# Transformer layer with dilated local attention and SwiGLU FFN: zero products at the start, one pass and the output additions moved, new list priorities

## Chip, cores and metric

The kernel runs on one core of one Trainium2 chip. The metric is the device time of one execution in microseconds; the time of a kernel is the median of its runs. In the text PE is TensorE, ACT ScalarE, DVE VectorE, POOL GpSimd, SP the engine that issues DMAs.

## What is computed

One pre-norm transformer layer in float32, on a sequence of 2048 positions of width 640:

```python
h  = x + attention(layernorm(x)) @ wo          # 32 heads of 20, wqkv 640 x 1920
h2 = h + (silu(n @ w_gate) * (n @ w_up)) @ w_down   # n = layernorm(h), F = 1728
# attention: position t sees t, t-2, ..., t-14 (8 keys, dilation 2), softmax over those 8
```

Every float32 product is made of three passes on PE: an operand is split into a high part, rounded to PE's fp32r format, and a remainder (the low part), and the kernel adds high x high, high x low and low x high.

## The kernel before

**Tiles.** The sequence is cut into four blocks b of 512 rows, each of 4 sub-blocks j of 128; the width into 5 chunks c of 128 and, for attention, into 4 groups g of 8 heads.

**Stages.** (1) The first layer norm of b (`ln1`, `LnStats`): for b = 0 the first three sub-blocks are normalized on DVE (`one_dve`, L266 to L276), the fourth on ACT; PE transposes them (L361), ACT copies the result as the high part (L363), DVE makes the low part (L364). For other b the same is done by `x_columns` and `to_columns` (L313, L316, L317). (2) `load_wqkv` brings the weights, with ACT making high parts (L374) and DVE remainders (L376). (3) `qkv`: 15 products per (b, g, j) into one of PSUM banks 0 to 4 (L400); ACT copies them out (L405), and SP stores q, k, v to scratch tensors in HBM (L411, L420). (4) Attention on DVE per (b, g): k, v, q windows are loaded (L435, L440); products and sums over a head (L448, L453), softmax (L460 to L474, with the exponential on ACT, L466), weighted sum of v (L479, L487), a turn (L494) and a store (L500). (5) `wo`: the output projection, per b eight groups of 15 products (L569), with its inputs split on ACT (L558) and DVE (L559), then the residual (L575, L580) and the second layer norm. (6) `ln2_columns`: the normalized rows are transposed into the tile `shb`, in five groups of four transposes that use banks 7, 6, 5, 7, 6 in turn; each group's bank is read by the high copy (L316) and by the low subtraction (L317). For b = 3 this goes through DMA (`ln2_turn`). (7) `ffn`: 14 tiles of 128 columns; `load_ffn` brings and splits weights (L606 to L624), `proj` makes gate (bank 5) and up (bank 6) in three passes of five products (L630), then silu, product and split on ACT and DVE (L661 to L665), and `do_down` adds the down product into banks 0 to 4 (L642). (8) `finish`: five additions on DVE from banks 0 to 4 into the residual (L692, L696) and the output DMAs (L700).

The tile `shb` holds the QKV inputs of b = 1 and 3 first and the FFN inputs later, so the FFN of b = 0 can take it only behind the last QKV products of b = 3.

**What sets the order.** Nothing is issued as written. Each step calls `P.add` with its engine, an assumed cost, the regions that it reads and writes and a priority; `Plan.order` plays a list schedule over all of them with those costs, and issues every engine's steps in the order found. The engine takes the ready step with the lowest priority number. The numbers stand in the table `PR` (L33) or in the calls; attention's DVE steps have 20, PE's products 10. For a step with priority 20 or more the planner looks whether a more urgent one will be ready soon, and if so leaves the engine idle until then (L92 to L96). On the chip each engine runs its list in order and waits by semaphores, so a step that is planned too early stalls those behind it.

The steps of `order` and of `proj` before:

```python
soon = min((a for a, m in pend[e] if ops[m][4] == 1), default=1e9)
...
for p, (w, a) in enumerate(((0, 0), (0, 1), (1, 0))):
    P.add("PE", 1.145, ..., r=[rr(gu + 1280 * w, wid * NC), ("shb", 2560 * a, 2560 * a + 2560)], w=[pb(bk)], prio=10)
```

Of the kernel before, what the change touches and what calls it, by code (L numbers as in the profile page):

```python
# [10 lines left out]
F32 = mybir.dt.float32  # L11
# [20 lines left out]
LAT, LAT0, RATE = 4.0, 2.0, 350e3  # L32
PR = {'x': 6, 'wqd': 2.5, 'wqh': 3, 'wql': 2.5, 'qev': 1, 'kvs': 3, 'atl': 3, 'exp': 8, 'ost': 0.5, 'wod': 6, 'woh': 3, 'wol': 2, 'old': 1, 'fld': 3, 'lst': 3, 'wev': 1, 'fh': 2, 'fl': 8, 'ln1': 6, 't1': 2, 'wo0': 1.5, 'wo': 2}  # L33


class Plan:
# [23 lines left out]
    def order(self):  # L60
# [15 lines left out]
        while todo:  # L76
# [15 lines left out]
            if prio >= 20:  # L92
                soon = min((a for a, m in pend[e] if ops[m][4] == 1), default=1e9)
                if soon < t + ops[n][1] - 0.3:
                    free[e] = soon
                    continue  # L96
# [23 lines left out]
def dve(n):  # L120
    return 0.155 + 0.00104 * n
# [13 lines left out]
def program(tc, x_in, wqkv_in, wo_in, ffn_in, ffl_in, const_in, out):  # L135
# [7 lines left out]
    with tc.tile_pool(name="sb", bufs=1) as sb, tc.tile_pool(  # L143
# [12 lines left out]
        def h_t():  # L156
            if "h" not in late:
                late["h"] = sb.tile([128, 5120], F32, name="h", tag="sha")
            return late["h"]
# [42 lines left out]
        def f(o, n):  # L202
            return fa[:, o : o + n]
# [7 lines left out]
        def rr(o, n):  # L211
            return ("ra", o, o + n)

        def pb(i):
            return (f"b{i}", 0, 1)
# [104 lines left out]
        XH = 13440  # L320

        def wq(g, half, k):
            return 4800 * g + 2400 * half + 480 * k
# [13 lines left out]
        def ln1(b):  # L337
# [4 lines left out]
            if b:  # L342
# [7 lines left out]
                return  # L350
            for j in range(NJ):
                (st.one_dve if j < 3 else st.one)(j)
                for c0, n, bk, bo in ((0, 4, 7 - j % 2, 0), (4, 1, 5, j)):
# [171 lines left out]
        def wo(b, prio, bks):  # L525
# [18 lines left out]
            if b:  # L544
                P.add("SP", 0.6, lambda: Q.dma_start(h_t()[:, h0 : h0 + 2560], x_in[b].rearrange("p j c -> p (j c)")),
                      w=[("sha", h0, h0 + 2560)], prio=PR["old"], nbytes=nb(512, 2560))
            for j in range(NJ):
                jp = j // 2
                for i in range(3) if j % 2 == 0 else ():
# [76 lines left out]

        def proj(bk, gu, col, wid):
            def mm(p, w, a):
                for c in range(NC):
                    T.matmul(banks[bk], r_(gu + 1280 * w + wid * c + col, 128), x2(a, c), start=p == 0 and c == 0, stop=p == 2 and c == NC - 1)  # L630
            for p, (w, a) in enumerate(((0, 0), (0, 1), (1, 0))):
                P.add("PE", 1.145, lambda p=p, w=w, a=a: mm(p, w, a), r=[rr(gu + 1280 * w, wid * NC), ("shb", 2560 * a, 2560 * a + 2560)], w=[pb(bk)], prio=10)

# [10 lines left out]
        def ffn(b):  # L644
# [8 lines left out]
            for i in range(NF):  # L653
# [4 lines left out]
                if i < NF - 1:  # L658
                    proj(5, gu, 0, 256)
                    proj(6, gu, 128, 256)  # L660
                    P.add("ACT", act(512), lambda so=so: A.activation(f(so, 512), banks[5], AF.Silu), r=[pb(5)], w=[rf(so, 512)], prio=0, table="silu")  # L661
# [5 lines left out]
                else:  # L667
                    proj(5, gu, 0, 128)
                    P.add("ACT", act(512), lambda so=so: A.activation(fa[64:128, so : so + 512], banks[5][0:64, :], AF.Silu), r=[pb(5)], w=[rf(so, 512)], prio=0, table="silu")
# [9 lines left out]
        def finish(b):  # L679
# [7 lines left out]
            for j in range(NJ):  # L687
                cuts = (0, 256, 512) if b == NB - 1 and j == NJ - 1 else (0, 512)
                pieces = list(zip(cuts, cuts[1:]))[::-1]
                for o, e in pieces:  # L690
                    lo, hi = hsl(b, j, o, e - o)
                    P.add("DVE", dve(e - o), lambda lo=lo, hi=hi, o=o, e=e, j=j: V.tensor_add(h_t()[:, lo:hi], banks[j][:, o:e], h_t()[:, lo:hi]), r=[pb(j), ("sha", lo, hi)], w=[("sha", lo, hi)], prio=0)  # L692
                    if j == 0:
# [30 lines left out]


        load_x(0, (0,))
        P.add("SP", 0.45, lambda: Q.dma_start(f(MASK, 160), const_in), w=[rf(MASK, 160)], prio=0, nbytes=nb(128, 640))
        load_x(0, (1,))
# [88 lines left out]
```

## Time and profile before

| | us |
|---|---|
| median of 3 runs | 869.96 (869.52 to 870.01) |
| the profiled execution's own time | 870.27 |
| its span, first to last instruction | 868.5 |
| PE busy | 855.7 |
| DVE busy | 641.7 |
| ACT busy | 401.4 |
| first PE instruction | 5.46 after the span's start |

The span is what the profile shows; the execution's time is 1.77 longer. Busy times are unions of the instructions' durations, so a PE that is 99% busy may still run its products at less than its pace: spacing from start to start is the better measure, and it is what the text uses. In the rows of the timeline the first number is the start in us from the span's start, the second how long the merged instructions took, then engine, line, operation, names, shape and count; in brackets the idle time before them and what ended it. "The chain" is the work followed back from the last instruction.

### The profile page before, as it was taken

What the parts mean: (1) busy time and instruction counts of PE and PEld (TensorE: products, weight loads), DVE (VectorE), ACT (ScalarE), POOL (GpSimd) and SP (SyncE); (2) the same over time, 40 slices, a digit from 0 to 9 for tenths busy, and PEclk for the clock granted to TensorE, in tenths of its full rate; (3) what the DMA queues carried; (4) which work ended last, traced back from release to release, by engine and by line L of the source; (5) the groups of instructions that cost most, each with busy time, mean ns of one, the idle gap of its engine ahead of it and who ended that gap; (6) DMA issues with size and microseconds to landing.
All of it is one profiled execution on the core that took longest, in us unless ns stands there. A gap on an engine that the chain in (4) does not pass through costs nothing.

```text
span 868.5 us, 10718 instructions
## 1 busy us (share of the span) xinstructions
PE 855.7 (99%) x4036; PEld 726.8 (84%) x4036; DVE 641.7 (74%) x743; ACT 401.4 (46%) x651; POOL 1.6 (0%) x7
## 2 busy tenths in 40 slices
PE   6999999999999999999999999999999999999998
PEld 5888888889978888888888888878988888888886
DVE  6489699999999999999999999995212116333332
ACT  5857732223682434574443567443464334333321
POOL 0000000000000000000000000000000000000000
PEclk9999999999999999999999999999999999999999
DMA  7995764596887969659997986887437645322201
GB/s 252 272 292 162 202 174 133 155 289 173 296 243 236 295 227 272 191 158 305 363 300 237 304 228 194 237 304 244 141 124 246 243 148 181 107 91 91 97 26 61
DMA packets 74612, 180.11 MB, mean 207 GB/s; under 512 B 28720, under 2 KB 39344, under 8 KB 73792
## 3 DMA queue, kind: packets, MB, share of 16 engines
q1 hardware_dynamic: 74560, 179.43, 65.6%
q8 instruction: 31, 0.51, 0.3%
q14 instruction: 21, 0.17, 0.1%
HBM read 138.36 MB, written 41.03 MB: 207 GB/s over the span
## 4 chain that ended last, share of the span: by engine, by line
PE 77%; DVE 18%; issue 2%; DMA 2%; SPq 0%; ACT 0%; DVEq 0%
PE bank L630 32%; PE bank L400 23%; PE bank L642 16%; PE bank L569 5%; DVE fa L487 3%; DVE fa L479 3%; DVE fa L448 3%; DVE fa L453 3%; PE bank L313 1%; DVE acts L665 1%; DVE fa L662 1%; DMA osc<-fa 1%; DVE fa L494 1%; DVE shb L317 1%; DMA fa<-in_x_dram 1%
## 5 line engine op out<-in xcount | busy, mean ns | idle before, releaser
L630 PE MATMUL bank<-shb,ra 128*128 128x512 f32 x1620 | 381.2, 390 | 2.3 <-DVE shb L317 2.1
L630 PEld LDWEIGHTS bank<-shb,ra 128*128 128x128 f32 x1620 | 303.1, 188 | 66.2 <-DVE shb L317 3.3
L642 PE MATMUL bank<-ra,acts 128*128 128x512 f32 x656 | 160.3, 391 | 0.0
L642 PEld LDWEIGHTS bank<-ra,acts 128*128 128x128 f32 x656 | 122.5, 188 | 25.1
L662 DVE TENSOR_TENSOR fa<-bank,fa 128x512 f32<-128x512 f32 x52 | 35.7, 687 | 129.2 <-PE bank L630 128.9
L400 PE MATMUL bank<-ra,sha 128*128 128x480 f32 x480 | 108.4, 385 | 0.0
L400 PE MATMUL bank<-ra,shb 128*128 128x480 f32 x470 | 104.7, 380 | 0.0
L400 PEld LDWEIGHTS bank<-ra,sha 128*128 128x128 f32 x480 | 91.4, 192 | 13.7
L607 ACT CAST ra<-fa 128x1280 fp32r<-128x1280 f32 (+1 forms) x56 | 68.8, 1229 | 66.4 <-PE bank L630 64.7
L400 PEld LDWEIGHTS bank<-ra,shb 128*128 128x128 f32 x470 | 87.5, 188 | 12.8
L479 DVE TENSOR_TENSOR fa<-fa 128x1280 f32<-128x1280 f32 x64 | 93.7, 1487 | 1.0
L448 DVE TENSOR_TENSOR fa<-fa 128x2560 f32<-128x2560 f32 x32 | 90.3, 2821 | 2.6 <-DMA fa<-qsc 2.1
L487 DVE TENSOR_TENSOR fa<-fa 128x1280 f32<-128x1280 f32 (+2 forms) x96 | 89.7, 935 | 2.7
L453 DVE TENSOR_REDUCE fa<-fa 128x128 f32<-128x2560 f32 x32 | 90.1, 2815 | 0.6
L405 ACT ACTIVATE st<-bank,fa 128x480 f32<-128x480 f32 x64 | 42.0, 658 | 84.8 <-PE bank L400 82.0
L661 ACT ACTIVATE fa<-bank 128x512 f32<-128x512 f32 x52 | 31.1, 598 | 107.7 <-PE bank L630 107.6
L624 DVE TENSOR_TENSOR ra<-fa,ra 128x640 fp32r<-128x640 f32 (+1 forms) x82 | 64.7, 817 | 16.2 <-ACT ra L608 14.0
L569 PE MATMUL bank<-ra 128*128 128x320 f32 x480 | 74.5, 309 | 0.0
L569 PEld LDWEIGHTS bank<-ra 128*128 128x128 f32 x480 | 72.4, 188 | 2.1
L608 ACT CAST ra<-fa 128x640 fp32r<-128x640 f32 x56 | 40.7, 728 | 63.0 <-PE bank L642 62.8
L663 ACT CAST acts<-fa 128x512 fp32r<-128x512 f32 x52 | 32.3, 621 | 49.5 <-DVE fa L662 49.4
L642 PE MATMUL bank<-acts,ra 128*128 128x512 f32 x164 | 46.3, 390 | 0.1
(82 smaller groups left out, 486.1 us busy)
## 6 DMA issues: line engine op xcount, KB each, us to landing
fa<-in_ffn_dram SPq DMA_DIRECT2D x52, 960.0 KB, 6.0
ra<-lsc SPq DMA_DIRECT2D x26, 640.0 KB, 5.4
fa<-ksc SPq DMA_DIRECT2D x32, 440.0 KB, 5.8
fa<-vsc SPq DMA_DIRECT2D x32, 440.0 KB, 5.8
ra<-lsc SPq DMA_DIRECT2D x30, 320.0 KB, 3.7
lsc<-ra SPq DMA_DIRECT2D x13, 640.0 KB, 5.1
ksc<-st SPq DMA_DIRECT2D x32, 160.0 KB, 4.4
qsc<-st SPq DMA_DIRECT2D x16, 320.0 KB, 3.5
```

Of the source, the lines that this page charges most:

```text
L400: T.matmul(banks[bk][:, 0:480], l, r_(wq(g, w, c), 480), start=(p, c) == first_mm, stop=(p, c) == last_mm)
L405: P.add("ACT", act(480) + 0.06, lambda bk=bk, j=j: A.activation(stage_t()[:, so : so + 1920].rearrange("p (t j c) -> p t j c", t=3, j=NJ)[ ...
L448: P.add("DVE", dve(2560), lambda: V.tensor_tensor(f(PROD, 2560).rearrange("p (j w c) -> p j w c", j=2, w=W), window(ko, 2 * jp), f(qo + 32 ...
L453: P.add("DVE", dve(2560), lambda: V.tensor_reduce(f(lo + 128 * jp, 128), f(PROD, 2560).rearrange("p (n d) -> p n d", d=DH), axis=AX.X, op= ...
L479: V.tensor_tensor(f(PROD + 1280 * jj, 1280).rearrange("p (w h d) -> p w h d", w=W, d=DH), f(vo + 160 * j, 1280).rearrange("p (w h d) -> p ...
L487: V.tensor_add(dst(v), v[:, :, 0:m, :], v[:, :, m : 2 * m, :])
L569: T.matmul(banks[bk][:, 0:320], l, r_(m, 320), start=p == 0 and c == 0, stop=p == 2 and c == NC - 1)
L607: P.add("ACT", act(n), lambda: A.copy(r_(gu, n), f(raw, n)), r=[rf(raw, n)], w=[rr(gu, n)], prio=PR["fh"])
L624: P.add(eng, c, lambda o=o: E.tensor_sub(ra[p0:, lo + o : lo + o + 640], fa[p0:, raw + o : raw + o + 640], ra[p0:, hi + o : hi + o + 640]. ...
L630: T.matmul(banks[bk], r_(gu + 1280 * w + wid * c + col, 128), x2(a, c), start=p == 0 and c == 0, stop=p == 2 and c == NC - 1)
L642: T.matmul(banks[k], l, m, start=first and p == 0, stop=last and p == len(passes) - 1)
L662: P.add("DVE", dve(512), lambda so=so: V.tensor_mul(f(so, 512), banks[6], f(so, 512)), r=[pb(6), rf(so, 512)], w=[rf(so, 512)], prio=0)
```

## The change

The change has five parts.

1. Zero products: POOL clears 128 columns of the weight tile `ra` (`WARM`), and PE multiplies them with themselves into bank 4: 20 products ahead of the first transposes, and 3 between the transposes of j = 0 and j = 1.
2. In the first tile (i = 0) of each FFN, up's first pass (high x high, bank 6) is issued behind gate's first pass, before gate's other two.
3. The output additions on DVE (L692) get priority 1.2 instead of 0 (the one from bank 4, L696, keeps 0).
4. The planner's look-ahead also counts steps of priority below 1, and steps that wait only for an ACT step that is itself ready or about to be.
5. Nearly all priorities of the table are new, and the last sub-block's steps of the output projection get 0.5.

```diff
-PR = {'x': 6, 'wqd': 2.5, 'wqh': 3, 'wql': 2.5, 'qev': 1, 'kvs': 3, 'atl': 3, 'exp': 8, 'ost': 0.5, 'wod': 6, 'woh': 3, 'wol': 2, 'old': 1, 'fld': 3, 'lst': 3, 'wev': 1, 'fh': 2, 'fl': 8, 'ln1': 6, 't1': 2, 'wo0': 1.5, 'wo': 2}
+PR = {'x': 0.4, 'wqd': 10, 'wqh': 10, 'wql': 10, 'qev': 6, 'kvs': 6, 'atl': 10, 'exp': 2.2, 'ost': 1, 'wod': 6, 'woh': 8, 'wol': 0.5, 'old': 6, 'fld': 4, 'lst': 10, 'wev': 3, 'fh': 1.2, 'fl': 0.4, 'ln1': 10, 't1': 1.5, 'wo0': 4, 'wo': 6}
...
-                soon = min((a for a, m in pend[e] if ops[m][4] == 1), default=1e9)
+                soon = min([a for a, m in pend[e] if ops[m][4] <= 1] + [
+                    max(free["ACT"], avail[d]) + ops[d][1] + 0.2
+                    for q in (ready["ACT"], pend["ACT"]) for _, d in q if ops[d][4] <= 1
+                    for m in succ[d] if ops[m][0] == e and ops[m][4] <= 1 and left[m] == 1], default=1e9)
...
+        WARM = XH + 1280
+
+        def warm(n, after=()):
+            def mm():
+                for _ in range(n):
+                    T.matmul(banks[4][:, 0:128], r_(WARM, 128), r_(WARM, 128), start=True, stop=True)
+            P.add("PE", 0.2 * n, mm, r=[rr(WARM, 128), *after], w=[pb(4)], prio=0)
...
             for j in range(NJ):
+                if j == 1:
+                    warm(3, [("b5", 0, 0.25)])
                 (st.one_dve if j < 3 else st.one)(j)
...
             for j in range(NJ):
+                if j == NJ - 1 and True:
+                    prio = stats.prio = 0.5
                 jp = j // 2
...
-        def proj(bk, gu, col, wid):
-            def mm(p, w, a):
+        def proj(bks, gu, wid, first):
+            passes = ((0, 0), (0, 1), (1, 0))
+
+            def mm(bk, col, p, w, a):
                 for c in range(NC):
                     T.matmul(banks[bk], r_(gu + 1280 * w + wid * c + col, 128), x2(a, c), start=p == 0 and c == 0, stop=p == 2 and c == NC - 1)
-            for p, (w, a) in enumerate(((0, 0), (0, 1), (1, 0))):
-                P.add("PE", 1.145, lambda p=p, w=w, a=a: mm(p, w, a), r=[rr(gu + 1280 * w, wid * NC), ("shb", 2560 * a, 2560 * a + 2560)], w=[pb(bk)], prio=10)
+            todo = [(n, p) for n in range(len(bks)) for p in range(3)]
+            if first:
+                todo.insert(1, todo.pop(3))
+            for n, p in todo:
+                w, a = passes[p]
+                P.add("PE", 1.145, lambda bk=bks[n], n=n, p=p, w=w, a=a: mm(bk, 128 * n, p, w, a), r=[rr(gu + 1280 * w, wid * NC), ("shb", 2560 * a, 2560 * a + 2560)], w=[pb(bks[n])], prio=10)
...
-                    proj(5, gu, 0, 256)
-                    proj(6, gu, 128, 256)
+                    proj((5, 6), gu, 256, i == 0)
...
-                    proj(5, gu, 0, 128)
+                    proj((5,), gu, 128, False)
...
-                    P.add("DVE", dve(e - o), lambda lo=lo, hi=hi, o=o, e=e, j=j: V.tensor_add(h_t()[:, lo:hi], banks[j][:, o:e], h_t()[:, lo:hi]), r=[pb(j), ("sha", lo, hi)], w=[("sha", lo, hi)], prio=0)
+                    P.add("DVE", dve(e - o), lambda lo=lo, hi=hi, o=o, e=e, j=j: V.tensor_add(h_t()[:, lo:hi], banks[j][:, o:e], h_t()[:, lo:hi]), r=[pb(j), ("sha", lo, hi)], w=[("sha", lo, hi)], prio=1.2)
...
+        P.add("POOL", 0.3, lambda: G.memset(r_(WARM, 128).bitcast(F32), 0.0), w=[rr(WARM, 128)], prio=0)
         load_x(0, (0,))
+        warm(20)
```

Lines in the text are those of the kernel before.

## Prediction

> **What bounds the kernel now.** I read the page first: busy times, TensorE's clock row, the chain that ended last. Then TensorE's own waits, then the timeline at every place where its spacing breaks.
>
> ```profile
> span 868.5 us, 10718 instructions
> ...
> PE 855.7 (99%) x4036; PEld 726.8 (84%) x4036; DVE 641.7 (74%) x743; ACT 401.4 (46%) x651; POOL 1.6 (0%) x7
> ...
> PE 77%; DVE 18%; issue 2%; DMA 2%; SPq 0%; ACT 0%; DVEq 0%
> ```
>
> ```profile
> PE bank L630 <- DVE shb L317: 2.1, 2, 1.4
> ```
>
> TensorE (PE) has work almost without a break. The DVE share of the chain lies where both engines are full, so it is not 18% to be won. What can be won is only time in which PE stands still or runs below its pace. Its pace, from the chain in order of time:
>
> ```profile
> 39.33 3.26 PE bank L400 x15
> 46.28 0.87 PE bank L313 x8
> 266.72 6.80 PE bank L630 x30
> ```
>
> That is 0.217 us for a QKV product, 0.109 for a transpose, 0.227 for an FFN product. Against this pace PE loses time at three places: the start, the way into the first FFN, and the way from the second FFN (b=1) to the third (b=2). The tail behind the last product is a fourth piece:
>
> ```profile
> 864.69 0.75 DVE L692 TENSOR_TENSOR h<-bank,h 128x256 f32<-128x256 f32 x2 [0.44 <-PE bank L642]
> ```
>
> The last product ends just ahead of them, at 864.65; then come two additions and their output DMAs, 3.85 us to the end of the span. The order of every engine from there on is the same in the changed kernel, so the tail counts as nothing. The new addition priority has nothing to compete with there.
>
> **The change part by part.** *The start: 20 zero products ahead of the first transposes, 3 between the first and the second group.*
>
> ```profile
> 5.46 1.33 PE L361 MATMUL bank<-fa 128*128 128x128 f32 x5 [5.46 <-DVE fa L275]
> ...
> 7.90 1.33 PE L361 MATMUL bank<-fa 128*128 128x128 f32 x5 [1.11 <-DVE fa L275]
> ...
> 8.88 6.83 PE L400 MATMUL bank<-ra,sha 128*128 128x480 f32 x20
> ...
> 12.56 0.55 DVE L275 TENSOR_SCALAR fa<-fa 128x640 f32<-128x640 f32 x1
> ...
> 14.46 0.65 DVE L376 TENSOR_TENSOR ra<-fa,ra 128x480 fp32r<-128x480 f32 x1
> ...
> 15.54 0.71 PE L361 MATMUL bank<-fa 128*128 128x128 f32 x5
> ...
> 16.18 0.75 ACT L363 CAST sha<-bank 128x512 fp32r<-128x512 f32 x2 [2.66 <-PE bank L361]
> ...
> 16.80 0.69 DVE L364 TENSOR_TENSOR sha<-bank,sha 128x512 fp32r<-128x512 f32 x1 [1.69 <-ACT sha L363]
> ...
> 17.42 4.83 PE L400 MATMUL bank<-ra,sha 128*128 128x480 f32 x21
> 17.91 0.65 DVE L376 TENSOR_TENSOR ra<-fa,ra 128x480 fp32r<-128x480 f32 x1
> ```
>
> ```profile
> 387.03 0.63 POOL L616 MEMSET ra<- 64x640 f32 x1 [133.00 <-PE bank L642]
> ```
>
> ```profile
> 9.42:13.42 4.00, 4.00 (x11) 3.30 (x10) 1.00 1.04 402
> ```
>
> The last fence is the windows view of line 400 alone: 4 us hold 10 products (the 11th only begins), 0.40 us each against 0.217 above. The clock column says 1.00, so the clock record misses the start; the durations show a half clock. It lasts until about 13.6 us, some 4.7 us after products began to follow each other at 8.88.
>
> The Trainium skill (TensorE: Matmul & The Clock Gate, Part 1) says that the array runs at half rate until a free-running window of about 3.4 us has been busy; 0.40 against 0.217 us agrees. An estimate from its figure: busy from 1.1 us on, the gate opens between 4.5 and 7.9 us. The sum below is the same by it.
>
> Price of a zero product: the trace has none. The nearest row is the cold transpose group, 128x128 too: from 7.90 to the next product at 8.88, five take 0.98 us, 0.196 each; the other end is the cold 480-column product, 0.40. I take 0.2, so 20 take 3.9 us (at 0.40: 8.0). They start behind a new POOL memset of 128x128, a fifth of the columns of the quoted 64x640 one of 0.63 us; with nothing ahead of it in the kernel, I put their start at 1.1, an estimate. They end at about 5.0 to 5.4; the first transposes wait for DVE until 5.46 anyway. The 3 others (0.6 us) lie in the pause from 6.5 to 7.9. Cover for all of it is DVE's wait for x. The result bank 4 is next used by a product after 20 us.
>
> With an open gate, step by step: the transposes at 7.90 take 0.55 instead of 0.98, so products begin at 8.45. Their inputs (the copies by ACT, DVE's first three remainders) come until 12 us, so the first 20 products end at about 13.2, with small waits. The third transposes need DVE's normalization, ready at 13.11 (12.56 + 0.55), which depends on nothing of PE: they start at 13.2 instead of 15.54. ACT then copies at 13.8 instead of 16.18, and DVE follows after its remainder of 14.46 to 15.11: 0.9 for the lower halves (0.69, and a quarter of the columns more), then the last weight remainder until 16.65 instead of 18.56. From 13.75 PE has 0.55 of transposes and 4 + 21 products of 0.217: 5.98, until 19.7, and the remainders (15.11, 16.65) arrive ahead of their users. In the profile the same 21 products end at 17.42 + 21 x 0.217 = 21.98. **Gain 2.2 us**; 0 if the gate opens no earlier, 2.5 (11 products x 0.18 and 5 transposes x 0.1) as the most. PE is the bound after this, so the lead is kept until it meets a wait.
>
> *Into the first FFN: up's first pass behind gate's first; other order of the subtractions.*
>
> ```profile
> 240.84:250.79 9.95, 8.29 (x42) 5.84 (x40) 9.78 (x15) 9.05 (x15) 0.00 (x0) 1.00 0.68 169
> ```
>
> ```profile
> 243.43 1.25 PE L400 MATMUL bank<-ra,shb 128*128 128x480 f32 x5
> ...
> 246.74 2.81 DVE L453 TENSOR_REDUCE fa<-fa 128x128 f32<-128x2560 f32 x1
> ...
> 249.46 1.28 DVE L317 TENSOR_TENSOR shb<-bank,shb 128x512 fp32r<-128x512 f32 x2
> ...
> 250.20 3.14 PE L630 MATMUL bank<-shb,ra 128*128 128x512 f32 x11 [1.40 <-DVE shb L317]
> ```
>
> The window holds 20 transposes, 15 QKV and 6 FFN products: 2.18 + 3.26 + 1.36 = 6.80 of 9.95 us, so 3.15 are lost. The cause stands in the rows: a 2.81 us reduction of the attention began just before the two subtractions (L317) that gate's second pass needs. In the new order the first four transposes groups stand earlier among the QKV groups, all five ahead of the last one, and no attention operation stands on DVE between the third and the fifth subtraction (the wider look-ahead in the planner holds DVE back). After the last read of the lower half (5 products, ending at 244.5 here) two subtractions remain, 1.28 us. Cover: the last 5 QKV products, 1.09, and gate's first pass, 1.14. Up's first pass writes bank 6, which the fifth transposes also used, so it too waits for the fifth subtraction; with 1.28 against 2.23 us it shouldn't wait. I leave 0.75 us for switches between transposes and products and for late starts: **gain 2.4**. Ends: 3.1 (nothing lost) and 0.5 (a long operation still in front, so that bank 6 is late too and only the earlier transposes help).
>
> *From b=1 to b=2: output additions behind the next columns.*
>
> ```profile
> 563.18 1.74 PE L313 MATMUL bank<-fa 128*128 128x128 f32 x12
> ...
> 567.77 1.64 PE L630 MATMUL bank<-shb,ra 128*128 128x512 f32 x6
> 570.06 2.12 PE L630 MATMUL bank<-shb,ra 128*128 128x512 f32 x8 [0.65 <-DVE shb L317]
> ```
>
> ```profile
> 566.23 1.89 DVE L692 TENSOR_TENSOR h<-bank,h 128x512 f32<-128x512 f32 x3
> 568.12 0.69 DVE L696 TENSOR_TENSOR h<-bank,h 128x512 f32<-128x512 f32 x1
> 568.73 0.68 DVE L692 TENSOR_TENSOR h<-bank,h 128x512 f32<-128x512 f32 x1
> 569.33 0.68 DVE L317 TENSOR_TENSOR shb<-bank,shb 128x512 fp32r<-128x512 f32 x1
> ```
>
> From 563.18 to 570.06 PE has 12 transposes, the last 10 down products, 4 more transposes and 6 products of the next FFN: 16 x 0.109 + 16 x 0.227 = 5.4 of 6.9 us, so 1.5 are lost. Five additions (3.1 us, 566.23 to 569.33) stand ahead of the one subtraction that PE waits for. Moved behind it, they free banks that the next down product writes only some 13 us later (4 groups of 15 at 0.227), so nothing is late for them. Their output DMAs start some us later, with 290 us left. ```profile
> L479 DVE TENSOR_TENSOR fa<-fa 128x1280 f32<-128x1280 f32 x64 | 93.7, 1487 | 1.0
> ```
>
> In total 20.9 us of DVE work (2 attention operations of 2.82, 6 of 1.49, smaller ones, the additions) now stands behind this point instead of ahead. What remains is read from the same change of b one FFN earlier:
>
> ```profile
> 403.62 1.47 PE L313 MATMUL bank<-fa 128*128 128x128 f32 x12
> ...
> 408.29 3.02 PE L630 MATMUL bank<-shb,ra 128*128 128x512 f32 x12
> ```
>
> There 16 transposes and 13 products, 4.7 us, fill 4.67: nothing lost. I take **1.2**; ends 0 and 1.5.
>
> *The other priorities.* The counts of products (but for the 23), table loads (31) and DMA issues (516) stay; they only move. What could be late next is the first output projection (L569), which in the profile starts just behind its input:
>
> ```profile
> 101.19 0.17 DVE L286 TENSOR_SCALAR fa<-fa 128x4 f32<-128x4 f32 x1 [3.65 <-ACT fa L263]
> ...
> 105.07 0.64 DVE L472 TENSOR_REDUCE fa<-fa 128x32 f32<-128x256 f32 x1 [2.78 <-ACT fa L466]
> ...
> 195.81 0.42 DVE L559 TENSOR_TENSOR ra<-fa,ra 128x256 fp32r<-128x256 f32 x1
> ...
> 197.31 8.96 PE L569 MATMUL bank<-ra 128*128 128x320 f32 x60
> ```
>
> Slack is 197.31 - 196.23 = 1.1 us. The new order puts 6.3 us more of attention ahead of that subtraction (3 of 1.49, three smaller), but also ends the two idle stretches of DVE above, 6.4 us, since the newton steps and the exponential no longer stand in front of ready work. Both engines start from the lead of 2.2 us, so the slack stays near 1.1. I count 0, with 0 to 3 lost as the bounds.
>
> **Sum.** 2.2 + 2.4 + 1.2 = 5.8 us off the profiled execution: span 868.5 to 862.7, its time 870.27 (1.77 more than its span) to 864.5. The median of the runs, 869.96, lies 0.3 below the profiled one, so 864.2.
>
> **The rivals.** *The gate doesn't open early* (the change doesn't do what it says at the start). For: in the profile, transposes at 5.46 and 7.90 with products from 8.88 did not open it before 13.6, though PE was busy for 1 us of the first 3 and then for all from 7.90; zero products end at 5.4 and a pause follows until 7.9 with 0.6 us of filler. Against: 4 us without pause is longer than any stretch that failed to open it. The start's 2.2 falls away: 866.4. The Trainium skill (the same page, Part 4) says that transposes don't count as busy for the gate; by that rule only the zero products count, and it is this rival. No row here tells transposes and products apart.
>
> *Zero products are dear* (0.40 each): they end at 9.1, the first transposes are 3.6 us late, products begin near 10 instead of 8.45, though at full clock; the later remainders slip by 1.2. The start gives 1.0: 865.4.
>
> *New waits eat it.* With DVE or loads a few per cent slower than planned, the first output projection waits up to 3 us, and 1 to 2 are lost elsewhere: 868.5 to 869.5, no change.
>
> *Slower: attention's loads come late.* Their priority is now the lowest on SP's queue (10), behind weights and stores, and SP issues in order.
>
> ```profile
> fa<-ksc SPq DMA_DIRECT2D x32, 440.0 KB, 5.8
> ```
>
> If two of the first five attention blocks each wait a whole landing, 11.6 us, less the slack of 1.1, L569 stands 10.5 us late and all behind it: 874.7. It decides from 1.1 + 5.8 us of lateness on. Against: in the new order the first loads of K, Q and V stand within one or two issues of where they stood, behind the same stores.
>
> **How the numbers follow.** The forecast 0.62 (own range 862.8 to 865.4), the closed gate 0.18, dear products 0.07, new waits 0.06, slower 0.07. A measurement tells 0.2% (1.7 us) from no change: faster is below 868.2, which the first three are: 0.87; same 0.06, slower 0.07. The range goes from 862.6 (all three gains at their upper ends, 7.1, and 0.3 for the spread between runs, 869.52 to 870.01) to 867.2, the closed gate with 0.8 less at the FFNs: it leaves out the last two cases and the edges.
>
> **What would show it.** Right: products of 0.217 from 8.5 us on, third transposes near 13.2, line 400's 21 products ending near 19.7; no reduction before the last two subtractions near 245, and no wait of the FFN products for them; additions behind the columns near 560; L569's first group without a wait. Wrong: 0.40 spacing beyond 9 us, the first transposes after 5.6, a wait before the first output projection, or PE waiting for bank 6 in up's first pass.

## The result, and the profile after

The kernel after takes **865.21 us** (median of 5 runs, 864.34 to 866.48) against 869.96 before (869.41 to 871.01 in the runs beside it): a ratio of 0.9946, 95% interval 0.9932 to 0.9959. The prediction was 864.2, with 862.6 to 867.2 as its range. The profiled execution took 865.21 too, 1.78 more than its span.

Lines from here on are those of the kernel after, unless a kernel is named. What was L313, L316, L317, L361, L400, L453, L569, L630, L642, L692 before is now L316, L319, L320, L376, L415, L468, L586, L649, L665, L714; the zero products are L331.

The page of the kernel after: span, busy times, the chain that ended last by engine.

```profile
span 863.4 us, 10743 instructions
...
PE 857.4 (99%) x4059; PEld 731.0 (85%) x4059; DVE 645.4 (75%) x743; ACT 402.4 (47%) x651; POOL 1.8 (0%) x8
...
PE 98%; DVE 1%; DMA 1%; ACT 0%; SPq 0%; issue 0%; DVEq 0%; ACTq 0%
```

PE's waits after (total, times, longest, in us):

```profile
PE bank L331 <- POOL ra L748: 1.0, 1, 1.0
PE bank L665 <- DVE acts L694: 0.6, 1, 0.6
PE bank L376 <- DVE fa L278: 0.5, 1, 0.5
```

PE's busy time rose by 1.7 us while the span fell by 5.0, so the share of busy time says nothing here. The chain says more: DVE's part fell from 18% to 1%. The wait for L317 (2.1 us) is gone, and a short new one for L694 stands in the list. Where the 5.0 us came from shows when the same product is set side by side in both traces, the 30th gate or up product of the first tile of each FFN:

| start of | before | after | lead | won since the row above | predicted |
|---|---|---|---|---|---|
| third transposes (j = 2) | 15.54 | 14.67 | 0.87 | 0.87 | 2.2 |
| 30th product, b = 0 | 256.13 | 252.03 | 4.10 | 3.23 | 2.4 |
| 30th product, b = 1 | 415.00 | 410.92 | 4.08 | -0.02 | 0 |
| 30th product, b = 2 | 575.41 | 569.79 | 5.62 | 1.54 | 1.2 |
| 30th product, b = 3 | 732.30 | 727.26 | 5.04 | -0.58 | 0 |
| end of the last product | 864.65 | 859.61 | 5.04 | 0 | 0 |

*Start.* PE's timeline after:

```profile
1.00 4.53 PE L331 MATMUL bank<-ra 128*128 128x128 f32 x20 [1.00 <-POOL ra L748]
5.49 1.33 PE L376 MATMUL bank<-fa 128*128 128x128 f32 x5
6.47 0.88 PE L331 MATMUL bank<-ra 128*128 128x128 f32 x3
7.89 1.33 PE L376 MATMUL bank<-fa 128*128 128x128 f32 x5 [0.54 <-DVE fa L278]
8.87 5.96 PE L415 MATMUL bank<-ra,sha 128*128 128x480 f32 x20
14.67 0.49 PE L376 MATMUL bank<-fa 128*128 128x128 f32 x3
```

Everything up to 7.89 is as foreseen: 20 zero products at 0.213 us from 1.00 on, the transposes of j = 0 not late. But the second transposes and the first products start where they stood before, 7.89 and 8.87 against 7.90 and 8.88, and 20 products take 5.96 us where full pace needs 4.3. From start to start they are 0.400 us until 11.8 us: the half clock ends 1.9 us earlier than before (11.91 against 13.77 in the trace's record of the clock), but not ahead of the products at 8.5, as the forecast needed.

*First FFN:* PE and DVE.

```profile
241.76 0.60 PE L316 MATMUL bank<-fa 128*128 128x128 f32 x4
242.12 1.33 PE L415 MATMUL bank<-ra 128*128 128x480 f32 x5
242.68 0.68 DVE L320 TENSOR_TENSOR shb<-bank,shb 128x512 fp32r<-128x512 f32 x1
...
243.77 0.69 DVE L320 TENSOR_TENSOR shb<-bank,shb 128x512 fp32r<-128x512 f32 x1 [0.41 <-PE bank L415]
...
244.37 1.25 PE L415 MATMUL bank<-ra 128*128 128x480 f32 x5
244.64 0.69 DVE L320 TENSOR_TENSOR shb<-bank,shb 128x512 fp32r<-128x512 f32 x1 [0.17 <-PE bank L415]
...
245.45 4.92 PE L649 MATMUL bank<-shb,ra 128*128 128x512 f32 x21
...
248.38 2.82 DVE L468 TENSOR_REDUCE fa<-fa 128x128 f32<-128x2560 f32 x1
```

Before, the 2.81 us reduction stood ahead of the last two subtractions, and PE stood from 248.8 to 250.2. Now the last transposes end ahead of the last 15 QKV products, DVE waits a little for PE (0.41, 0.17) with nothing long in front of its three subtractions, the last is done at 245.33, and 21 FFN products run in 4.92 us without a break. The reduction comes after.

*From b = 1 to b = 2:*

```profile
558.42 1.47 PE L316 MATMUL bank<-fa 128*128 128x128 f32 x12
560.14 1.88 DVE L320 TENSOR_TENSOR shb<-bank,shb 128x512 fp32r<-128x512 f32 x3
...
561.94 1.28 DVE L714 TENSOR_TENSOR h<-bank,h 128x512 f32<-128x512 f32 x2
563.09 3.24 PE L649 MATMUL bank<-shb,ra 128*128 128x512 f32 x13
```

The subtractions are done at 562.02, a microsecond before the first product; the additions follow them.

*From b = 2 to b = 3*, the one place that became worse (the last fence is PE before, at the same place):

```profile
714.64 1.66 ACT L733 CAST shb<-fa 128x512 fp32r<-128x512 f32 x3
714.89 0.69 DVE L692 TENSOR_TENSOR fa<-bank,fa 64x512 f32<-64x512 f32 x1
715.61 0.82 DVE L641 TENSOR_TENSOR ra<-fa,ra 128x640 fp32r<-128x640 f32 x1
716.32 0.62 ACT L693 CAST acts<-fa 64x512 fp32r<-64x512 f32 x1
717.07 0.69 DVE L694 TENSOR_TENSOR acts<-fa,acts 64x512 fp32r<-64x512 f32 x1
717.81 0.73 PE L665 MATMUL bank<-acts,ra 128*128 128x512 f32 x2 [0.63 <-DVE acts L694]
```

```profile
722.60 1.64 PE L630 MATMUL bank<-shb,ra 128*128 128x512 f32 x5
```

The last FFN tile's split (L692, L693, L694) must be done before its down products. It comes late, and 0.8 us from start to start is lost there (over the whole FFN the kernel after loses 0.58 us more than before). The new order put no other PE work in front, while before five products of the next FFN ran there.

### The profile page after: what moved, and what is told of

The parts are those of the page before. It is cut to its first block, busy times and chain, and to the rows that moved or that the text cites. A ratio compares the mean times of both kernels' runs of the same rounds, so it can differ in the third digit from the quotient of the medians.

```text
span 863.4 us, 10743 instructions
## 1 busy us (share of the span) xinstructions
PE 857.4 (99%) x4059; PEld 731.0 (85%) x4059; DVE 645.4 (75%) x743; ACT 402.4 (47%) x651; POOL 1.8 (0%) x8
## 4 chain that ended last, share of the span: by engine, by line
PE 98%; DVE 1%; DMA 1%; ACT 0%; SPq 0%; issue 0%; DVEq 0%; ACTq 0%
PE bank L649 42%; PE bank L415 24%; PE bank L665 21%; PE bank L586 8%; PE bank L316 2%; DMA fa<-in_x_dram 1%; PE bank L376 0%; PE bank L707 0%; DVE ra L641 0%; ACT ra L624 0%; DVE fa L276 0%; DVE acts L694 0%; DVE fa L692 0%; DVE shb L734 0%; DVE fa L278 0%
## 5 line engine op out<-in xcount | busy, mean ns | idle before, releaser
L649 PE MATMUL bank<-shb,ra 128*128 128x512 f32 x1620 | 378.9, 389 | 0.0
L649 PEld LDWEIGHTS bank<-shb,ra 128*128 128x128 f32 x1620 | 303.3, 188 | 62.2 <-ACT fa L683 0.2
L665 PE MATMUL bank<-ra,acts 128*128 128x512 f32 x656 | 160.5, 391 | 0.0
L665 PEld LDWEIGHTS bank<-ra,acts 128*128 128x128 f32 x656 | 122.4, 188 | 25.1
L415 PE MATMUL bank<-ra,sha 128*128 128x480 f32 x480 | 107.6, 383 | 0.0
L415 PE MATMUL bank<-ra,shb 128*128 128x480 f32 x470 | 104.9, 380 | 0.0
L415 PEld LDWEIGHTS bank<-ra,sha 128*128 128x128 f32 x480 | 90.7, 190 | 13.5
L415 PEld LDWEIGHTS bank<-ra,shb 128*128 128x128 f32 x470 | 87.4, 188 | 12.8
L468 DVE TENSOR_REDUCE fa<-fa 128x128 f32<-128x2560 f32 x32 | 90.1, 2816 | 0.7
L641 DVE TENSOR_TENSOR ra<-fa,ra 128x640 fp32r<-128x640 f32 (+1 forms) x82 | 64.8, 818 | 17.5 <-ACT ra L625 15.0
L586 PE MATMUL bank<-ra 128*128 128x320 f32 x480 | 74.5, 309 | 0.0
L586 PEld LDWEIGHTS bank<-ra 128*128 128x128 f32 x480 | 72.4, 188 | 2.1
L665 PE MATMUL bank<-acts,ra 128*128 128x512 f32 x164 | 46.4, 391 | 0.6 <-DVE acts L694 0.6
```

What stands on the lines that cost most here:

```text
L415: T.matmul(banks[bk][:, 0:480], l, r_(wq(g, w, c), 480), start=(p, c) == first_mm, stop=(p, c) == last_mm)
L468: P.add("DVE", dve(2560), lambda: V.tensor_reduce(f(lo + 128 * jp, 128), f(PROD, 2560).rearrange("p (n d) -> p n d", d=DH), axis=AX.X, op= ...
L586: T.matmul(banks[bk][:, 0:320], l, r_(m, 320), start=p == 0 and c == 0, stop=p == 2 and c == NC - 1)
L641: P.add(eng, c, lambda o=o: E.tensor_sub(ra[p0:, lo + o : lo + o + 640], fa[p0:, raw + o : raw + o + 640], ra[p0:, hi + o : hi + o + 640]. ...
L665: T.matmul(banks[k], l, m, start=first and p == 0, stop=last and p == len(passes) - 1)
```

## The experiments

The kernel before, run beside the experiments, took 870.05, 869.95 and 870.18 us (medians of 15 to 17 runs, 868.54 to 871.51).

**What the zero products do.** The theory: products of 128 columns don't fill PE enough to open the clock, and the 0.87 us at the start is chance. Rivals: the zeros are too quiet as data, or the products did help.

`e1_after_no_zero_products`: the kernel after, its 23 products not issued.

```diff
-                for _ in range(n):
-                    T.matmul(banks[4][:, 0:128], r_(WARM, 128), r_(WARM, 128), start=True, stop=True)
+                pass
```

> The changed kernel with the 23 zero products left out (the planner still reckons with them, so every other instruction keeps its place). Theory phase: the narrow zero products never open the clock; it opens at the first boundary of a free-running 3.41 us window behind dense wide products, and the 0.9 us that the changed kernel won at the start is the luck of that phase. Then this one is like the changed kernel, 864.3 to 866.5 us, and the 0.40 us spacing ends anywhere between 11.9 and 15.3 us. Theory help: they bring the clock forward. Then it is slower by 0.9 to 2 us, 866 to 867.5.

Measured: 865.67 us (865.34 to 866.82), ratio 0.9954 (0.9942 to 0.9966), not to be told from the kernel after. Its profiled execution is the slowest of its five (866.82). In it the third transposes start at 13.75, 0.9 earlier than with the zero products, and near 114 PE waits once 1.8 us for a subtraction that the kernel after has in time:

```profile
PE bank L316 <- DVE shb L320: 1.8, 1, 1.8
```

The missing products are not what makes that subtraction late. In this execution DVE waited 2.33 and 1.38 us for the loads of two of the first attention blocks (starts at 42.23 and 58.88), against 0.81 and 0.17 in the profile after, and it stayed late until there. In `e6`, whose third transposes start at 13.74 too, DVE waits 0.99 us for the first of these loads and not for the second, and PE's wait near 114 isn't there.

`e2_after_ones`: the same 23 products, of ones.

```diff
-G.memset(r_(WARM, 128).bitcast(F32), 0.0)
+G.memset(r_(WARM, 128).bitcast(F32), 1.0)
```

> The changed kernel with ones instead of zeros as the operands of the 23 extra products. Theory data: the clock does not count products of zeros; with ones it opens by 5 to 8 us, products have 0.217 us spacing from 8.5 us on, and the time falls by 1 to 1.5 us to about 864. Theory width (128-column products leave the array idle half of the time, whatever the data) and theory phase: no difference from the changed kernel, 864.3 to 866.5.

Measured: 865.29 us (864.53 to 866.91), ratio 0.9949 (0.9937 to 0.9961); third transposes at 14.70, as after. It isn't whether the data are zeros or ones.

`e4_before_plus_zero_products`: the kernel before with the 20 and 3 products and the memset.

> The kernel before with the zero products alone (POOL clearing, 20 and 3 products of 128 columns). Theory phase: no gain beyond the luck of the phase, 869 to 871 us. Theory help: 0.9 to 2 us less, 868 to 869.

Measured: 870.17 us (868.03 to 872.15, 11 runs), ratio 1.0 (0.9991 to 1.0009). Added alone, the zero products are worth nothing, to the 0.8 us that the interval allows.

`e3_after_wide_zeros`: 9 and 5 zero products of 512 columns in place of 20 and 3 of 128 (the memset clears as many columns; that line is left out here).

```diff
-                for _ in range(n):
-                    T.matmul(banks[4][:, 0:128], r_(WARM, 128), r_(WARM, 128), start=True, stop=True)
+                for _ in range(9 if n == 20 else 5):
+                    T.matmul(banks[4], r_(WARM, 128), r_(WARM, 512), start=True, stop=True)
```

> The changed kernel with 9 and 5 zero products of 512 columns in place of 20 and 3 of 128. Theory width: these stream without pause, a window from about 1.7 to 5.1 us is full and opens the clock at its end (or at the next boundary, 8.5 us, at the latest); the first real products have 0.217 us spacing, third transposes near 13.2 us, and the time falls by 1 to 1.5 us to about 864. Theory data: the clock stays at half as in the changed kernel, 865.2. Either way the first transposes may be late by up to 0.3 us.

Measured: 863.99 us (863.46 to 866.83, 6 runs), ratio 0.9937 (0.9925 to 0.995). PE's timeline:

```profile
1.32 4.21 PE L331 MATMUL bank<-ra 128*128 128x512 f32 x9 [1.32 <-POOL ra L748]
...
8.46 4.79 PE L415 MATMUL bank<-ra,sha 128*128 128x480 f32 x20
13.09 0.71 PE L376 MATMUL bank<-fa 128*128 128x128 f32 x5
```

This is the start that the prediction worked out: products from 8.46 (8.45 was written), at full pace, third transposes at 13.09 (13.2). With wide products the clock does open in time.

`e10_zeros_of_256_columns`: the same count as after, 20 and 3, with 256 columns (the memset's line is left out again).

```diff
-T.matmul(banks[4][:, 0:128], r_(WARM, 128), r_(WARM, 128), start=True, stop=True)
+T.matmul(banks[4][:, 0:256], r_(WARM, 128), r_(WARM, 256), start=True, stop=True)
```

> The kernel after, its 20 and 3 zero products taking 256 columns instead of 128. Theory (a narrow product leaves the array half idle, since weights for each of 128 columns take as long as the columns; what counts is columns): if 256 columns take the same 0.213 us as 128 did, the stretch counts as full and the clock opens near 5.1 or before the first products at 8.5: third transposes near 13.1, 20 QKV products in 4.8 us, 864.0. Rival (products of zeros below 512 columns don't count): products at 0.400 from 8.5 to 11 or later, third transposes near 14.5, 865.2. If a product takes 0.43 us instead, the first transposes start late, at about 9.6.

Measured: **863.51 us** (863.15 to 864.23), ratio 0.9924 (0.9912 to 0.9937), the fastest kernel here: its slowest run lies below the fastest of the kernel after (864.34). PE's timeline:

```profile
1.10 4.64 PE L331 MATMUL bank<-ra 128*128 128x256 f32 x20 [1.10 <-POOL ra L748]
...
7.77 4.95 PE L415 MATMUL bank<-ra,sha 128*128 128x480 f32 x20
12.56 0.71 PE L376 MATMUL bank<-fa 128*128 128x128 f32 x5
```

Twice the columns, and the same 0.213 us from start to start: at half clock a product of 128 columns takes as long as one of 256. This is the cleanest pair, since count, place and spacing are those of the kernel after, and the one opens the clock (at 6.58) and the other doesn't (11.91). The start gains 2.98 us at the third transposes (15.54 to 12.56), more than the 2.2 that was forecast, because DVE's normalization of j = 2 also comes earlier. Part of that is chance: in this execution DVE begins the statistics of j = 1 at 5.47 without a wait, while before it waited for the load of x and began at 6.12.

**Which part moved the order.** The prediction gave the first FFN to the earlier transposes and the planner, and b = 1 to b = 2 to the additions' priority.

`e5_after_gate_passes_first`: `proj((5, 6), gu, 256, False)`, so that gate's three passes come first again.

> The kernel after, but gate's three passes come ahead of up's in the first tile of each FFN, as before; DVE's and ACT's orders are the same as after. Theory (the order of the transposes and of DVE's subtractions ends the wait before the first FFN, and the moved pass adds cover that is not needed): the last two subtractions (1.3 us) lie behind the last five QKV products (1.1) and gate's first pass (1.1), so gate's second pass is 0 to 0.3 us late at each change of b; the time stays within 0.5 us of the kernel after's 865.2. Rival (up's first pass is what covers the subtractions): the first FFN waits 1 us or more at gate's second pass, and the same again at b=1 and b=2: 866.2 to 868.

Measured: 865.12 us (864.43 to 865.85), ratio 0.9945 (0.9933 to 0.9958). PE has the same three waits as after and none at gate's second pass. The moved pass has no measurable worth in this order.

`e6_after_additions_at_0`: `prio=0` for the additions.

> The kernel after, but the output additions have priority 0 again. Theory of the prediction (the additions' priority moves them behind the columns from b=1 to b=2 and gives 1.2 us there): five additions stand again ahead of the last subtraction near 560, PE waits there some 1.3 us, 866.5. Rival (there the order comes from the table and the look-ahead; the priority decides only from b=2 to b=3): nothing near 560 changes, PE waits 1.5 to 2.5 us near 717 instead of the 0.8 that the kernel after shows at that place: 866 to 867, all of the difference at 717.

Measured: 865.68 us (864.59 to 867.25), ratio 0.9954 (0.9941 to 0.9966). From b = 1 to b = 2 all is as after: the subtractions at 559.20, the additions behind them at 561.00, no wait. The difference stands from b = 2 to b = 3:

```profile
719.74 3.15 PE L649 MATMUL bank<-shb,ra 128*128 128x512 f32 x13
...
720.16 1.28 DVE L714 TENSOR_TENSOR h<-bank,h 128x512 f32<-128x512 f32 x2
...
722.82 1.29 DVE L734 TENSOR_TENSOR shb<-fa,shb 128x512 fp32r<-128x512 f32 x2
723.56 11.37 PE L649 MATMUL bank<-shb,ra 128*128 128x512 f32 x47 [0.67 <-DVE shb L734]
```

Additions (L714) stand ahead of the last subtractions (L734). 13 products last from 719.74 to 723.56, 3.82 instead of 2.95 us, and with the uneven spacing behind the wait the first 30 products of this FFN take 1.4 us more than after (8.00 for 6.59). The kernel after runs 60 products there without a break. The rival had the place right: with the new table and look-ahead the priority isn't needed from b = 1 to b = 2, and decides from b = 2 to b = 3. Its 866 to 867 was too much, and by time alone the two kernels can't be told apart, as the start of this execution fell 0.9 us earlier.

`e7_after_old_lookahead`: the planner's one-line look-ahead of before, all else as after.

> The kernel after with the planner's look-ahead of before; the table is the new one. Theory (the look-ahead holds DVE back ahead of the columns' subtractions, the table does the rest): a long attention operation stands again ahead of the last subtractions at the first FFN, PE loses 2.5 to 4 us there, and nothing at the other two changes of b: 868 to 869.5. Rival (the table alone puts the transposes early enough): less than 0.7 us lost at the first FFN, 865 to 866.

Measured: **873.46 us** (873.05 to 876.23), ratio 1.0049 (1.0036 to 1.0061): slower than before, and by more than either theory gave. The profiled execution is the slowest of its five (876.23). PE's longest wait, and the windows of its timeline behind it (length, busy time and instructions of each engine, then the granted clock):

```profile
PE bank L646 <- DVE shb L317: 3.7, 1, 3.7
```

```profile
250.46:253.87 3.41, 0.95 (x2) 0.83 (x3) 3.41 (x5) 0.58 (x1) 0.00 (x0) 0.50 0.67 236
253.87:257.29 3.42, 3.42 (x9) 2.64 (x8) 3.35 (x4) 0.00 (x0) 0.00 (x0) 0.50 1.02 246
257.29:260.70 3.41, 3.41 (x16) 2.82 (x15) 1.76 (x3) 1.50 (x2) 0.00 (x0) 1.00 0.96 372
```

The new table lets weight remainders (L638, 3.02 us) and attention's steps pass the last subtraction at the first FFN, PE stands for 3.7 us, and then its clock falls to a half for two stretches of 3.41 us (in the second 9 products run, in the stretch behind it 16). Another 1.4 us is lost at 114, where DVE was late from a wait of 2.86 us for attention's first load, as in `e1`; that piece can't be laid on the look-ahead. Smaller pieces are lost at 239 and 408.

From b = 1 to b = 2, though, this kernel without the wider look-ahead wins 1.12 us against before (159.29 us from the 30th product of the one FFN to that of the next, 160.41 before, 158.87 after), and its additions (L711) stand behind the last subtractions:

```profile
570.72 1.88 DVE L317 TENSOR_TENSOR shb<-bank,shb 128x512 fp32r<-128x512 f32 x3
572.51 0.68 DVE L711 TENSOR_TENSOR h<-bank,h 128x512 f32<-128x512 f32 x1
```

`e8_after_old_table`: the old table, all else as after.

> The kernel after with the table of priorities of before; the look-ahead, the pass and the additions are new. Theory (table and look-ahead are needed together): PE loses 1.5 to 2.5 us at the first FFN, since the transposes stand late among the QKV groups, and about 1 us from b=2 to b=3: 867 to 868.5. Rival (the look-ahead does all of it, the table is worth nothing): within 0.5 us of the kernel after, 865.2, or below it where the casts from b=2 to b=3 no longer stand in front of the last high copy: 864.6.

Measured: 868.85 us (867.46 to 870.05, 11 runs), ratio 0.9989 (0.998 to 0.9998). PE waits 1.9 us at the first FFN for a subtraction, behind a reduction as before, and loses clock there as well. From b = 2 to b = 3, where its theory looked for 1 us more, it loses nothing: its lead on the kernel before is 2.10 us at the 30th product of b = 2 and 2.13 at that of b = 3. So the place that became worse came with the new table. A window behind its wait, and a row of its start:

```profile
247.68:251.09 3.41, 3.41 (x9) 2.22 (x8) 3.41 (x6) 2.06 (x3) 0.00 (x0) 0.50 1.04 386
```

```profile
8.18 4.84 PE L415 MATMUL bank<-ra,sha 128*128 128x480 f32 x20
```

Here the narrow products stand as in the kernel after, and yet the QKV products run at full pace from the second on (see the last section).

`e12_before_with_lookahead`: the kernel before with the new look-ahead, nothing else.

> The kernel before with the new look-ahead alone, its table the old one. Theory (neither the table nor the look-ahead gives the gain alone; the kernel after with the old table took 868.85): 868.5 to 870, a wait of 1.5 to 2.5 us at the first FFN in transposes or subtractions, nothing lost near 560. Rival (the look-ahead alone gives most of it): 866 to 867.5.

Measured: 868.6 us (867.25 to 871.04, 11 runs), ratio 0.9985 (0.9976 to 0.9993). Its lines differ; L456 is the reduction, L633 the FFN product:

```profile
246.33 2.81 DVE L456 TENSOR_REDUCE fa<-fa 128x128 f32<-128x2560 f32 x1
...
249.06 1.28 DVE L320 TENSOR_TENSOR shb<-bank,shb 128x512 fp32r<-128x512 f32 x2
...
249.79 2.48 PE L633 MATMUL bank<-shb,ra 128*128 128x512 f32 x8 [1.40 <-DVE shb L320]
```

At the first FFN it is the kernel before, wait for wait. By the planner's code the look-ahead sees such a subtraction only when ACT's copy ahead of it is ready or about to be; that the old table's transposes are too late for that is read from the code, not shown by a run. From b = 1 to b = 2, though, it loses nothing, with the additions' priority still 0: subtractions at 563.66, additions at 565.49, and 1.31 us won between the 30th products. So the look-ahead alone is enough for most of that gain; by `e7` it isn't needed for it either, where the new table and the additions' priority are there.

`e11_before_with_table_and_lookahead`: the kernel before with new table, 0.5 for the last sub-block and new look-ahead; no zero products, old passes and additions.

> The kernel before with the new table (and the 0.5 for the last sub-block) and the new look-ahead; no zero products, passes and additions as before. Theory (these two together are the gain; zero products, passes and additions were each found worth 0.5 us or less): no wait of 1 us at the first FFN, nothing lost near 560, some 2 us lost near 717: 865.2 to 866.7. Rival (the zero products or the moved pass are needed to go with them): 867.5 or more.

Measured: 866.22 us (866.0 to 870.26, 6 runs), ratio 0.9961 (0.9947 to 0.9975). At the first FFN 21 products run in 4.95 us without a wait; near 723 PE waits as in `e6`. Of the 4.75 us of the whole change, 3.96 are here (870.18 less 866.22). Neither half does it: the look-ahead alone gives 1.6 us, and the kernel after loses 8.25 without it (873.46 less 865.21) and 3.64 without the new table. The 0.5 for the last sub-block was not run apart from the table.

**A remedy for the place that became worse.** `e9_wide_and_held_casts`: `e3`, and the last three casts of b = 3's columns held behind L693.

```diff
-r=[rf(XN + 512 * k, 512)], w=[hi(k)]
+r=[rf(XN + 512 * k, 512)] + ([("ab", 2048, 2560)] if k > 1 else []), w=[hi(k)]
```

> The kernel after with zero products of 512 columns, and with the last three of the five casts of b=3's columns (L733) held behind the high copy of b=2's last FFN tile (L693), by a read of the region that the copy writes. Theory (L693 stands behind three casts of 0.55 us on ACT, and PE waits for the subtraction L694 behind it): the 0.8 us lost near 716 falls to 0.2 or less, nothing else is late; 0.6 us less than the same kernel without the hold (863.99): 863.4. Rival (DVE is what makes L694 late, since L641 of 0.82 us stands between): the loss stays at 0.6 to 0.8 there, 864.0.

Measured: 864.28 us (863.85 to 864.59), ratio 0.9931 (0.9919 to 0.9943), no better than `e3`. ACT, DVE and PE in its profile:

```profile
714.21 0.83 DVE L641 TENSOR_TENSOR ra<-fa,ra 128x640 fp32r<-128x640 f32 x1
714.41 0.62 ACT L693 CAST acts<-fa 64x512 fp32r<-64x512 f32 x1
714.95 0.68 DVE L734 TENSOR_TENSOR shb<-fa,shb 128x512 fp32r<-128x512 f32 x1
...
715.67 0.69 DVE L694 TENSOR_TENSOR acts<-fa,acts 64x512 fp32r<-64x512 f32 x1
...
716.41 0.74 PE L665 MATMUL bank<-acts,ra 128*128 128x512 f32 x2 [0.63 <-DVE acts L694]
```

The copy L693 is done at 715.03, 0.6 us ahead of its user, and PE waits just as long: DVE has L641 and L734 in front of L694. My theory that the casts were to blame fell. What now stands in front is DVE's own order; a kernel that puts L694 ahead of L641 and L734 was not run, so that this is the cause is argued.

## Why the prediction was right, and where it wasn't

The time was right to 1.0 us, the sum of the span to 0.8 (5.0 for 5.8). The terms were less right than their sum, and that it came so near is in part luck: the start fell 1.33 us short, two other terms gave 1.17 more than forecast, and 0.58 was lost where nothing was looked for.

- **The start (2.2 predicted, 0.87 measured) is the step that failed.** PE's chain of work was right, as `e3` shows: first products at 8.46, third transposes at 13.09, the 21 products done at 19.65, where 8.45, 13.2 and 19.7 were written. The price (0.2, measured 0.213) and the end (5.0 to 5.4, measured 5.5 with the last) were right too. What failed is "4 us without pause is longer than any stretch that failed to open it". The prediction's own reading stood against it, 4.7 us of products from 8.88 on at half clock. And PE busy in time was not enough: 20 products of 128 columns without pause did not open the clock, 20 of 256 at the same spacing did. Its estimate that the gate opens between 4.5 and 7.9 us held for the wide products (6.58 in `e10`, 7.20 in `e3`), not for these (11.91). The rival "the gate doesn't open early" is what happened, at a chance of 0.18. It gave 866.4; less the 0.87 that the start won after all, and with the other three terms as measured (0.83 and 0.34 more, 0.58 less), it is 864.9.
- The 0.87 can't be put down to the zero products. Kernels with the narrow ones have their third transposes anywhere from 12.86 (`e8`) to 14.90 (`e5`), those without any from 13.75 (`e1`) to 15.54 (before): where the first full stretch falls differs from one execution to the next. The stretch that opened the clock after, 8.50 to 11.91, holds none of the zero products (the last section works it out).
- The Trainium skill (TensorE: Matmul & The Clock Gate, Part 1) says that the window is free-running and that the place of the opening so varies from run to run; these starts agree. The Trainium skill's rule in Part 4 of the same page, that transposes don't count as busy, was cited for the rival. `e8` speaks against it: between 5.33 and 8.75 it has mostly transposes (54% of the time) and 12% QKV products, and its clock was open at 8.75 (the row at 8.18 under that experiment). The narrow products failed here for another reason than that rule.
- **First FFN (2.4 predicted, 3.23 measured): right in mechanism.** Transposes ahead, no reduction ahead of the subtractions, no wait; `e7` and `e8` show that the look-ahead and the table are both needed for it. The 0.75 us left for switches and late starts was too much: from 240.84 to 250.79 products and transposes at full pace now fill 9.8 of 9.95 us, and the gain is all of the 3.15 that the prediction found lost. Up's first pass was counted as cover; `e5` shows that gate's alone is enough.
- **From b = 1 to b = 2 (1.2, measured 1.54): right in size and mechanism, too narrow in cause.** The additions do stand behind the subtractions. The prediction gave that to their priority alone; `e6` and `e12` show that it isn't needed where the wider look-ahead is, and `e7` that the look-ahead isn't needed where the new table and the priority are (1.12). Whether the priority would do it by itself was not run.
- **Other priorities (0, with up to 3 lost): 0.58 lost**, from b = 2 to b = 3, a place at which the prediction did not look. The first output projection, where the loss was looked for, starts without a wait at 193.21, and attention's loads held up DVE less than before (0.81 and 0.17 us at two of its first blocks, 1.74 and 0.36 before). That the rival "attention's loads come late" is possible shows in `e1`, where such waits cost PE 1.8 us. The additions' priority earns 1.4 us at this same change of b, by `e6`.
- **Tail (0): 0.03** (3.85 us from the end of the last product to that of the span before, 3.82 after).

What the prediction said would show it wrong did show: spacing of 0.40 beyond 9 us. Its other signs (first transposes after 5.6, a wait before the output projection or for bank 6) did not.

## What to carry to other kernels

Filler work that is to open PE's clock should be tried wide: the same 20 products at the same places opened it with 256 columns and not with 128, for the same time on PE. A table of priorities and the rule that applies it are one change: the table that, with the new look-ahead, is part of a gain of 4 us leaves the kernel 3.5 us slower than before with the old one, so test them together and apart. An effect that one change suffices for need not be its alone: leave each candidate out as well as putting it in. When a wait has two candidates in front of it on two engines, read the order of the engine that ends last before mending the other.

## What the runs showed of the hardware

**The clock moves in steps of 3.413 us.** The trace records the granted clock, the share of full speed at which PE may run. Its full clock lasts 853.33 us before and 849.92 after, which differ by 3.41; the half clock inside `e4` and `e8` lasts 3.413, inside `e7` 6.83. All are whole multiples of 3.4133 (250, 249, 1 and 2). The record begins with the opening of the clock (13.77 before, 11.91 after); ahead of it the spacing of the products tells that it is at half. Laying steps of this length back from each opening over the first 14 us, a step opens the clock by what PE did in it. The table gives shares of the step; an instruction counts until the next one starts, and at most with its own steady spacing at half clock:

| kernel, step | narrow products | transposes | wide zeros or QKV | opened |
|---|---|---|---|---|
| after, 1.67 to 5.09 | 1.00 | 0 | 0 | no |
| after, 5.09 to 8.50 | 0.26 | 0.43 | 0 | no |
| `e4`, 4.74 to 8.15 | 0.36 | 0.53 | 0 | no |
| `e7`, 4.70 to 8.11 | 0.37 | 0.48 | 0 | no |
| before, 6.94 to 10.36 | 0 | 0.27 | 0.39 | no |
| `e12`, 6.49 to 9.90 | 0 | 0.35 | 0.35 | no |
| `e8`, 5.33 to 8.75 | 0.19 | 0.54 | 0.12 | yes |
| `e1`, 7.22 to 10.63 | 0 | 0.27 | 0.65 | yes |
| `e3`, 3.79 to 7.20 | 0 | 0.27 | 0.65 | yes |
| `e10`, 3.16 to 6.58 | 0 | 0.27 | 0.73 | yes |

The first row is not one execution's accident: in all six (after, `e2`, `e4`, `e5`, `e7`, `e8`) in which narrow products filled a whole step, it stayed shut. If a narrow product counts half and a transpose in full, every step with 0.71 or less stays shut and every one with 0.76 or more opens; any weight of a narrow product from 0.21 to 0.76 parts them as well. That 256 columns do what 128 don't is measured; the half and the bounds are a fit, and no run tests them by themselves. Why a narrow product counts for less stays open. Its width alone doesn't say it, since a transpose has 128 columns and takes 0.213 us too, and `e8` needs it to count for more.

**A short wait can cost clock as well.** In `e4`, `e7` and `e8` the clock fell to 0.50 for one, two and one steps behind waits of 1.4 to 3.7 us at the first FFN. The steps ahead of the fall had PE at work for 0.40, 0.36 and 0.28 of their time (counted at full pace). Steps of 0.41 in `e1`, at 113, of 0.49 in `e7`, at 114, and of 0.55 and 0.59 before, at 246 to 253, did not make it fall; with 0.40 and 0.41 on two sides this is no tested threshold. The Trainium skill (TensorE: Matmul & The Clock Gate, Part 1) lets the clock fall after an idle window of about 3.4 us; here steps that were 28 to 40% busy were enough, and the measurement decides. A closed step costs about 1.6 us (8 products at 0.427 instead of 0.227 in `e4`). So a wait of 2 us in a stretch that otherwise runs full can have a second price.

The profile before doesn't show this price, but its other runs do. Profiled executions with no closed step have a mean granted clock of 0.999 or 1.0, those with one (`e4`, `e8`) 0.998. Of the 49 runs of the kernel before beside the experiments, 31 have 0.997 or 0.998; all five of the kernel after have 0.999 or 1.0, and all five of `e7` have 0.995 to 0.998. The 31 have a median of 870.18 us and the other 18 one of 869.78, so little of the 4.75 us is this.
